# Weight conversion through PSUM, a third raw weight buffer, and a rearranged start in a fused attention and MoE kernel

## The chip, the cores and the metric

The kernel runs on one core of a Trainium2 chip. The time is the device time of one execution in microseconds. Three timed executions of the kernel before gave 914.54, 918.44 and 958.26 us; the median, 918.44 us, is the time before. The profile is of one further execution, which took 917.19 us.

## The reference

The kernel computes bucketed attention over 2 batches of 8 heads, 768 positions and 64 dimensions, and then two MoE-like layers with the same shapes, the second on the output of the first. Cut to what is computed:

```
q_bits = (q @ proj > 0); k_bits = (k @ proj > 0)            # 6 bits per position
mask   = bucket(q_bits) == bucket(k_bits)
scores = where(mask, q @ k.T / 8, -1e9)
attn   = exp(scores - max);  attn = attn / (sum(attn) + 1e-9)
x      = (attn @ v), heads side by side                      # 1536 x 512
h      = x @ w_in;  x = (s * relu(h)**2 + b) @ w_out         # w_in 512 x 2048
h      = x @ w2_in; out = (h * clip(h + 3, 0, 6) / 6) @ w2_out
```

q, k, v and proj come as float32. The four weight matrices come as float64 (8 bytes per element, 2 x 16 tiles of 128 x 512 for each layer), and the kernel itself turns them into float32.

## The kernel before, in words

**Precision.** Every operand of a matmul is split into a high part (a cast, on ACT) and a low part (a subtraction, on POOL or DVE), and three products are added. So each weight tile is cast (w_hi, L653, ACT), subtracted (w_lo, L659, POOL) and then used by twelve matmuls of 384 columns (mm, L681).

**Attention.** The work is cut into 4 units (batch, half of the queries) of 4 head pairs, 16 pairs g in all, and each pair into 6 slots. For a pair, k and q are loaded (load_k, load_q), cast (k_hi, q_hi, q_top) and split (k_lo, q_lo on POOL). The bucket bits of k and q are found by a small matmul (bits_mm, L381) and a comparison on DVE (bits, L390). The k bits are scaled by a large number on ACT (bits_big, L396), stored to DRAM (bits_out, L402), and fetched from there into rows 64 to 75 of the operand KA (bits_in, L413); the q bits go straight into QA in two small DMAs (L406). Rows 64 to 127 of QA and KA are first filled with 0 and 1 (ones_rows, L328 and L329, POOL). Score tiles S (qk, L460) are reduced to a row maximum by DVE (smax, L468). When a pair's twelve maxima are there, the transposed scores T are computed (st, L520), exponentiated and split (texp, t_hi on ACT, t_lo on POOL), multiplied with v (pv_mm, L549) and summed (den_mm, L560). The first unit's four pairs are loaded at the start of the program.

**The two layers.** There are 8 jobs of 32 weight tiles: both layers for each of the four units. In a job the first 16 tiles (the lower half) each make one block of the hidden layer: a PSUM bank is filled by 12 matmuls, then read by a chain of four steps that alternate between ACT and DVE (g_relu L692, g_prod L698, g_hi L705, g_lo L713 for the first layer; L700, L707, L716 stand in it for the second), and the bank is free when g_lo has ended. The last 16 tiles (the upper half) fill one bank per four tiles. Accumulators rotate over three banks: one of the ring mm, two of the ring mmx (function mring); the ring mm also holds the small matmuls' results of the first unit.

**The conversion.** In jobs 0 and 1 each weight tile is loaded raw (w_load, L613, 512 KB, two buffers wr), and made float32: ACT scales the upper words into a buffer wm (w_exp, L619) and writes the low half-words of the result wf (w_ends, L631), DVE writes the sign bits (w_ends, L633) and joins wm into wf (w_join, L638). wf is stored to DRAM (w_store, L644, 256 KB) and used; jobs 2 to 7 fetch it from there (L648). A raw buffer is free when L619, L631 and L633 have read it.

**What sets the order.** A planner in the program (class Plan) lists all steps with engine, expected duration, needs and buffer rings, and writes one fixed order for each engine's queue and for the DMA queue of SP (some DMAs go to ACT's queue). On the chip each engine works through its order and waits at the first step that isn't ready. A table of constants (P_BUFS ... AHEAD, WARM) and the durations in the add calls steer the planner.

**The warming block.** warm (L374) issues matmuls of 512 columns on a tile `idle` of zeros that nobody reads; WARM says how many.

Of the kernel before, what the change touches and what calls it, by code (L numbers as in the profile page):

```python
# [20 lines left out]
NB = 6  # L21
# [6 lines left out]
P_BUFS, PT_BUFS, WF_BUFS, WS_BUFS, WR_BUFS, WM_BUFS, AHEAD = 2, 3, 4, 3, 2, 1, 7  # L28
WARM = 8
# [196 lines left out]
def attn_moe_moe2(ctx, tc, qT, kT, vT, proj, cvec, eye, w1_in, w1_out, w2_in, w2_out, out):  # L226
# [21 lines left out]
    wm_p = ctx.enter_context(tc.tile_pool(name="wm", bufs=WM_BUFS))  # L248
# [18 lines left out]
    idle = const.tile([128, 512], F16, name="idle")  # L267
# [6 lines left out]
    eyes = const.tile([128, 390], F32, name="eyes")  # L274
    ident, own_slot = eyes[:, 0:128], eyes[96:96 + 2 * SPP, 384:390]
# [219 lines left out]
    def u_rows(g):  # L495
        fl = sm_p.tile([128, 128], F32, tag="fl", name="fl")
        nc.scalar.copy(fl[96:114], pd[g]["nr"][96:114, 0:128])
        pd[g]["fl"] = fl
# [118 lines left out]
    def w_exp(key):  # L617
        mt = wm_p.tile([128, 512], I32, tag="wm", name="wm")
# [111 lines left out]
    def o_store(j, d, key):  # L730
# [7 lines left out]
                 "vt": 4, "iv": 4, "pvs": 1, "U": 1, "ds": 1, "kH": 1, "qD": 1, "kHx": 1, "qDx": 1, "nx": 3, "nh": 2, "cols": 2, "fl": 3,  # L738
                 "o": 2, "r": 2, "wr": WR_BUFS, "wm": WM_BUFS, "wf": WF_BUFS, "wh": WS_BUFS, "wl": WS_BUFS})
# [35 lines left out]
    for g in range(NP):  # L775
# [15 lines left out]
        for nm in "kq":  # L791
            if nm == "q" or own:
# [7 lines left out]
                else:  # L800
                    add("ACT", t, 0.48, bits_big, (g,), needs=[("bits", g, nm)], gives=[("big", g)])
                    add("DMA", t, (0.45, 0.55), bits_out, (g, nm), needs=[("big", g)], gives=[("ks", g)], rel=[(o, (nm, g))])
# [175 lines left out]
```

## Time and profile before

| | |
|---|---|
| timed executions | 914.54, 918.44, 958.26 us |
| profiled execution | 917.19 us, its span 915.4 us |
| PE busy | 845.7 us, 92% of the span |
| ACT, POOL, DVE busy | 591.8, 593.5, 510.4 us |
| DMA | 136.71 MB, mean 149 GB/s |

The span is the stretch of the profiled execution from the first to the last instruction; the 1.8 us between it and the execution's time lie around it. Busy time of an engine is the sum of its instructions, and the rows of the section on the trace give it for stretches of the span. PE means the matmuls. The share of granted TensorE clock (PEclk) is 1.00 at full speed. The chain that ended last leads from the last instruction back to the first, at each step to what that step had waited for.

### The profile page before, as it was taken

How to read it: one execution, taken by the hardware profiler on the slowest of the kernel's cores; microseconds unless marked ns; L12 is line 12 of the kernel's file. 1: busy time of each engine (PE TensorE's matmuls, PEld its weight loads, DVE VectorE, ACT ScalarE, POOL GpSimd, SP SyncE). 2: the span in 40 equal slices, each digit the busy share in tenths (PEclk: the TensorE clock that was granted, in tenths of full speed). 3: DMA queues.
4: the chain of work that ended last, by engine and by line, in shares of the span. 5: the costliest groups of instructions: out<-in, count | busy, mean ns of one | idle time of the engine just before them, and what ended most of it. 6: DMA issues, size and time to landing. Idle time of an engine off the chain costs nothing.

```text
span 915.4 us, 15214 instructions
## 1 busy us (share of the span) xinstructions
PE 845.7 (92%) x5416; PEld 745.2 (81%) x5416; DVE 510.4 (56%) x845; ACT 591.8 (65%) x993; POOL 593.5 (65%) x396
## 2 busy tenths in 40 slices
PE   4998776997789989899999999999999999999998
PEld 1666456896778877899899887999988787999998
DVE  3688676889798878682554434540474532530520
ACT  5288757886898876475468575663777464753752
POOL 9387633587475777367757878566687665666664
PEclk9999899998898999899999999999999999999999
DMA  9634567778875575855533434344342222444342
GB/s 210 149 79 138 139 215 228 243 249 259 256 227 190 186 210 158 201 159 133 127 113 107 129 100 124 122 128 127 120 127 79 78 67 73 134 128 127 118 143 74
DMA packets 74843, 136.71 MB, mean 149 GB/s; under 512 B 20144, under 2 KB 30736, under 8 KB 74768
## 3 DMA queue, kind: packets, MB, share of 16 engines
q1 hardware_dynamic: 72834, 131.99, 49.1%
q10 hardware_dynamic: 1934, 3.76, 1.6%
q8 instruction: 42, 0.69, 0.3%
q14 instruction: 33, 0.27, 0.1%
HBM read 104.15 MB, written 21.54 MB: 137 GB/s over the span
## 4 chain that ended last, share of the span: by engine, by line
PE 72%; DMA 11%; DVE 9%; ACT 5%; issue 2%; SPq 1%; POOL 1%; ACTq 0%; DVEq 0%; POOLq 0%
PE mm L681 49%; PE S L460 7%; DMA wr<-w_in 6%; PE T L520 6%; PE pv L549 5%; DMA wr<-w_out 2%; DVE wf L638 1%; DVE nh L468 1%; PE S L560 1%; DVE wf L633 1%; ACT wf L631 1%; PE pv L581 1%; PE S L381 1%; DMA vP<-v_t 1%; ACT wm L619 1%
## 5 line engine op out<-in xcount | busy, mean ns | idle before, releaser
L659 POOL TENSOR_TENSOR wl<-wf,wh 128x512 fp32r<-128x512 f32 x256 | 339.9, 1330 | 223.8 <-ACT wh L653 182.1
L681 PE MATMUL mm<-X,wh 128*128 128x384 f32 x1024 | 271.6, 346 | 20.8 <-DVE G L713 13.0
L681 PE MATMUL mm<-G,wh 128*128 128x384 f32 x1024 | 269.5, 344 | 0.0
L653 ACT CAST wh<-wf 128x512 fp32r<-128x512 f32 x256 | 157.6, 617 | 93.0 <-PE mm L681 65.3
L539 POOL TENSOR_TENSOR pt<-P,pt 128x768 f16<-128x768 f32 x96 | 162.1, 1693 | 81.6 <-ACT pt L533 78.0
L681 PEld LDWEIGHTS mm<-X,wh 128*128 128x128 f32 x1024 | 189.1, 194 | 30.8 <-DVE G L713 17.1
L681 PEld LDWEIGHTS mm<-G,wh 128*128 128x128 f32 x1024 | 183.0, 188 | 13.9 <-issue 12.0
L681 PE MATMUL mm<-X,wl 128*128 128x384 f32 x512 | 175.1, 342 | 0.0
L681 PE MATMUL mm<-G,wl 128*128 128x384 f32 x512 | 173.1, 338 | 0.0
L468 DVE TENSOR_REDUCE nh<-S 128x1 f32<-128x384 f32 x192 | 103.9, 551 | 84.6 <-PE S L460 83.8
L526 ACT ACTIVATE P<-T 128x768 f32<-128x768 f32 x96 | 77.8, 810 | 40.5 <-PE T L520 36.3
L681 PEld LDWEIGHTS mm<-X,wl 128*128 128x128 f32 x512 | 99.1, 194 | 0.0
L681 PEld LDWEIGHTS mm<-G,wl 128*128 128x128 f32 x512 | 96.3, 188 | 0.4 <-POOL wl L659 0.4
L533 ACT CAST pt<-P 128x768 f16<-128x768 f32 x96 | 79.6, 831 | 7.6 <-PE pv L549 5.5
L460 PE MATMUL S<-KA,QA 76*128 76x384 f32 x192 | 75.5, 393 | 7.9 <-DVE nh L468 6.6
L638 DVE SCALAR_TENSOR_TENSOR wf<-wm,wf 128x512 int32<-128x512 int32 x64 | 66.2, 1034 | 14.9 <-ACT wm L619 12.9
L520 PE MATMUL T<-QA,KA 108*128 108x384 f32 x192 | 69.7, 363 | 3.9 <-ACT P L526 3.8
L631 ACT ACTIVATE wf<-wr 128x512 uint16<-128x512 uint16 x64 | 50.8, 794 | 31.2 <-issue 12.4
L460 PE MATMUL S<-KB,QB 128*128 128x384 f32 x192 | 69.3, 361 | 0.0
L549 PE MATMUL pv<-pt,vt 128*64 128x384 f16 x576 | 64.1, 345 | 4.6 <-DVE wf L638 4.5
L520 PE MATMUL T<-QB,KB 128*128 128x384 f32 x192 | 66.7, 348 | 0.0
L633 DVE TENSOR_SCALAR wf<-wr 128x512 uint16<-128x512 uint16 x64 | 57.8, 903 | 14.6 <-issue 5.9
(357 smaller groups left out, 975.4 us busy)
## 6 DMA issues: line engine op xcount, KB each, us to landing
wf<-w SPq DMA_DIRECT2D x188, 256.0 KB
wr<-w_in SPq DMA_DIRECT2D x32, 512.0 KB
wr<-w_out SPq DMA_DIRECT2D x32, 512.0 KB
w<-wf SPq DMA_DIRECT2D x63, 256.0 KB
KB<-KA SPq DMA_DIRECT2D x16, 384.0 KB
qD<-q_t SPq DMA_DIRECT2D x28, 192.0 KB
kH<-k_t SPq DMA_DIRECT2D x13, 384.0 KB
U<-ur SPq DMA_DIRECT2D x15, 192.0 KB
```

What stands on the lines that cost most here:

```text
L460: nc.tensor.matmul(out=sp[:, 0:NQ], lhsT=operand(g, Q)[0:n, h, 128 * t:128 * t + 128], rhs=operand(g, K)[0:n, h, NQ * j:NQ * j + NQ], star ...
L468: nc.vector.reduce_max(out=pd[g]["nh"][:, j, c:c + 1], in_=sd.pop((s, j))[:, 0:NQ], axis=AX.X, negate=True)
L520: nc.tensor.matmul(out=tp[:, j, 0:NQ], lhsT=operand(g, K)[0:n, h, c:c + 128], rhs=operand(g, Q)[0:n, h], start=(a == 0), stop=(a == 1))
L526: nc.scalar.activation(out=P, in_=td.pop((g, k))[:, :, 0:NQ], func=AF.Exp, scale=0.125)
L533: (nc.scalar.copy if THI(g) == "ACT" else nc.vector.tensor_copy)(pd[g][h][:, 0, 2 * i:2 * i + 2], pd[g]["P", k])
L539: e.tensor_tensor(out=pt[:, 1, 2 * i:2 * i + 2], in0=pd[g].pop(("P", k)), in1=pt[:, 0, 2 * i:2 * i + 2], op=ALU.subtract)
L549: nc.tensor.matmul(out=d["pv"][64 * h:64 * h + 64, 0:NQ], lhsT=vt[:, vc, 64 * h:64 * h + 64], rhs=d[h][:, a, c], start=(c == 0 and n == 0) ...
L633: nc.vector.tensor_scalar(out=f16[:, :, 1], in0=r16[:, :, 3], scalar1=0x8000, scalar2=None, op0=ALU.bitwise_and)
L638: nc.vector.scalar_tensor_tensor(out=wf, in0=wq[key]["mt"], scalar=3, in1=wf, op0=ALU.logical_shift_left, op1=ALU.bitwise_or)
L653: nc.scalar.copy(hi.rearrange("p a b -> p (a b)"), wq[key]["wf"])
L659: nc.gpsimd.tensor_tensor(out=lo.rearrange("p a b -> p (a b)"), in0=d["wf"], in1=d["hi"].rearrange("p a b -> p (a b)").bitcast(F32), op=AL ...
L681: nc.tensor.matmul(out=a, lhsT=w[:, k, :], rhs=src[k][:, xi, :], start=(k0 + k == 0 and p == 0), stop=(k0 + k == nk - 1 and p == 2))
```

## The change

Five things are changed.

- w_exp writes the scaled upper words into a PSUM bank of the ring mm in place of the SBUF buffer wm, which is gone. Accumulators of jobs 0 and 1 use the two banks of mmx alone; from job 2 on all three rotate as before.
- The raw weights have three buffers.
- For the first four pairs the k bits go from the tile `bits` straight into KA, in four DMAs of 12 x 384 words. They are still stored to DRAM, later, for the second unit with the same keys.
- The warming block comes in two parts, 16 matmuls after the first pair's bits and 6 after the second's, and works on the tile `eyes` in place of a tile of zeros.
- The constant rows of QA and KA are set by DVE in place of POOL.

The small buffer fl has one copy in another pool, the release of iv moves to a later step, and several durations that the planner assumes for DMAs and for w_join are changed, which reorders the program.

```diff
-P_BUFS, PT_BUFS, WF_BUFS, WS_BUFS, WR_BUFS, WM_BUFS, AHEAD = 2, 3, 4, 3, 2, 1, 7
-WARM = 8
+P_BUFS, PT_BUFS, WF_BUFS, WS_BUFS, WR_BUFS, AHEAD = 2, 3, 4, 3, 3, 7
+WARM = (16, 6)
...
-    idle = const.tile([128, 512], F16, name="idle")
+    idle = eyes.bitcast(F16)[:, 0:512]
...
     def ones_rows(e):
-        nc.gpsimd.memset(sets[e]["QA"][64:128].bitcast(F32), 0.0)
-        nc.gpsimd.memset(sets[e]["KA"][64:128].bitcast(F32), 1.0)
+        nc.vector.memset(sets[e]["QA"][64:128].bitcast(F32), 0.0)
+        nc.vector.memset(sets[e]["KA"][64:128].bitcast(F32), 1.0)
...
     def bits_in(g):
         u, hp = pairs[g]
+        if g < 4:
+            dst = operand(g, "KA").rearrange("p h n -> p (h n)").bitcast(F32)
+            for i in range(4):
+                queue[0].dma_start(out=dst[64:64 + 2 * NB, 384 * i:384 * i + 384], in_=pd[g]["kbt"][32 * i:32 * i + 2 * NB].bitcast(F32))
+            return
...
     def w_exp(key):
-        mt = wm_p.tile([128, 512], I32, tag="wm", name="wm")
+        mt = ps["mm"].tile([128, 512], F32, tag="mm", name="wm").bitcast(I32)
...
+    CONV = max(min(n for n, job in enumerate(jobs) if job[0] == m) for m in range(2))
+
     def mring(key):
         jn, i = key
         n = 20 * jn + (i if i < 16 else 12 + i // 4)
-        return "mm" if n % 3 == 2 else "mmx"
+        return "mm" if jn > CONV and n % 3 == 2 else "mmx"
...
-    add("PE", -80.0, 0.22 * WARM, warm, (WARM,), needs=[("qmm", 1), ("kmm", 1)], acq=[("pv", "w")], rel=[("pv", "w")], soon=-80.0)
+    for i, n in enumerate(WARM):
+        add("PE", -80.0, 0.22 * n, warm, (n,), needs=[("kmm", i), ("qmm", i)], acq=[("pv", ("w", i))], rel=[("pv", ("w", i))], soon=-80.0)
     for e in range(4):
-        add("POOL", e - 4.0, 1.4, ones_rows, (e,), gives=[("ones", e)])
+        add("DVE", 9.0 * e - 14.0, 2.0, ones_rows, (e,), gives=[("ones", e)])
...
-                add("DMA", tw - 4.0, (0.45, 1.46), w_load, (m, i, ck), needs=use, acq=[(wr, ck)], gives=[("wr",) + ck])
+                add("DMA", tw - 4.0, (0.6, 2.2), w_load, (m, i, ck), needs=use, acq=[(wr, ck)], gives=[("wr",) + ck])
...
-                add("DVE", tw, 1.09, w_join, (ck,), needs=[("we",) + ck, ("wd", 1) + ck], gives=[("wf",) + ck],
+                add("DVE", tw, 0.66, w_join, (ck,), needs=[("we",) + ck, ("wd", 1) + ck], gives=[("wf",) + ck],
```

**Order at the start, SP's queue.** Of before first (kb is the tile in DRAM that the k bits pass through, KB<-KA a copy within the operands, kH and kHx raw keys, qD and qDx raw queries, vP raw values):

```order
L355 DMA KB_153<-KA_151 64x1536
L355 DMA KB_157<-KA_155 64x1536
L402 DMA kb_121<-bits 128x384
L406 DMA QA_152<-bits 12x384 x2
L334 DMA kH<-k_t 64x1536
L342 DMA qD<-q_t 64x2x384 x2
L413 DMA KA_151<-kb_121 12x4x384
L402 DMA kb_122<-bits 128x384
```

And of the change:

```order
L354 DMA KB_149<-KA_147 64x1536
L413 DMA KA_147<-bits 12x384 x4
L405 DMA QA_148<-bits 12x384 x2
L333 DMA kH<-k_t 64x1536
L401 DMA kb_117<-bits 128x384
L354 DMA KB_153<-KA_151 64x1536
```

The fetch of the first pair's k bits stood behind a store and three loads; its four pieces now stand behind one copy, ahead of the q bits, and the store follows the next key load.

**Order at the start, DVE.** Of the change, where before only five small memsets stood ahead of the first bits (QA and KA are the operands of the first unit's pairs):

```order
L327 MEMSET QA_148 64x768
L328 MEMSET KA_147 64x1536
L327 MEMSET QA_152 64x768
L328 MEMSET KA_151 64x1536
L327 MEMSET QA_159 64x768
L328 MEMSET KA_158 64x1536
L389 TENSOR_SCALAR bits<-small,cv 128x384
L327 MEMSET QA_163 64x768
L328 MEMSET KA_162 64x1536
L389 TENSOR_SCALAR bits<-small,cv 64x384
L423 TENSOR_REDUCE am<-vP 128x1
```

Three pairs of memsets stand ahead of the first k bits and a fourth ahead of the first q bits.

**Order at the first raw loads, SP's queue.** Of before (ur and U are small tiles of the attention, w_0 the first converted tile in DRAM):

```order
L613 DMA wr<-w_in 128x1024 [waits DMAHW3_49]
L613 DMA wr<-w_in 128x1024 [waits DMAHW4_49]
L501 DMA ur_132<-fl 6x128 [waits DMAHW5_49,Activation_49]
L334 DMA kH<-k_t 64x1536 [waits DMAHW6_49,Pool_49]
L505 DMA U<-ur_131 128x1x384 [waits DMAHW7_49,DVE_49]
L613 DMA wr<-w_in 128x1024 [waits DMAHW0_49,DMAHW3_49,DVE_49,Activation_49]
```

And of the change:

```order
L617 DMA wr<-w_in 128x1024 [waits DMAHW1_49]
L617 DMA wr<-w_in 128x1024 [waits DMAHW2_49]
L617 DMA wr<-w_in 128x1024 [waits DMAHW3_49]
L509 DMA U<-ur_126 128x1x384 [waits DMAHW4_49,DVE_49]
```

Three raw loads now go out before one waits for DVE and ACT to have read a buffer; before there were two.

## Rows read from the trace of the kernel before

**Rows 1.** The page: PE's busy tenths in 40 slices; the chain by line.

```profile
PE   4998776997789989899999999999999999999998
PE mm L681 49%; PE S L460 7%; DMA wr<-w_in 6%; PE T L520 6%; PE pv L549 5%; DMA wr<-w_out 2%; DVE wf L638 1%; DVE nh L468 1%; PE S L560 1%; DVE wf L633 1%; ACT wf L631 1%; PE pv L581 1%; PE S L381 1%; DMA vP<-v_t 1%; ACT wm L619 1%
```

**Rows 2.** Busy time by stretch: PE, PEld, DVE, ACT, POOL, clock, DMA share, GB/s.

```profile
22.00:46.00 24.00, 23.83 (x72) 14.86 (x73) 16.27 (x36) 6.98 (x11) 9.86 (x5) 1.00 0.69 148
46.00:108.00 62.00, 56.67 (x450) 41.16 (x448) 49.15 (x92) 51.27 (x71) 48.92 (x28) 0.94 0.40 105
108.00:120.00 12.00, 6.54 (x89) 3.83 (x90) 6.42 (x10) 5.70 (x11) 6.04 (x4) 0.86 0.89 245
120.00:175.00 55.00, 41.75 (x211) 37.41 (x211) 41.26 (x72) 41.63 (x78) 20.18 (x14) 0.97 0.68 225
207.00:230.00 23.00, 17.95 (x144) 15.64 (x145) 21.14 (x24) 15.14 (x24) 17.77 (x10) 0.87 0.77 247
230.00:300.00 70.00, 58.52 (x338) 53.16 (x337) 58.77 (x94) 60.48 (x107) 39.58 (x25) 0.92 0.71 229
```

**Rows 3.** The same view of L631 alone (one per weight tile): ACT, clock, DMA.

```profile
120.00:175.00 55.00, 11.95 (x15) 0.97 0.68 225
230.00:300.00 70.00, 14.24 (x18) 0.92 0.71 229
```

**Rows 4.** The chain in order of time: start us, us, what.

```profile
11.02 0.52 ACT bits L396
...
16.61 4.93 DMA KA<-kb
...
21.78 1.62 PE S L460 x4
...
41.51 1.65 PE T L520 x4
...
44.44 2.41 PE T L520 x8
...
64.77 0.91 PE S L460 x4
...
191.53 2.12 PE mm L681 x12
```

**Rows 5.** The timeline at the start: start us, us, engine, line, what.

```profile
0.87 0.27 DVE L914 MEMSET idle<- 128x256 uint32 x1 [0.87 <-PEq L971]
6.89 0.62 DVE L390 TENSOR_SCALAR bits<-small,cv 128x384 fp32r<-128x384 f32 x1 [5.45 <-PE small L381]
8.88 3.44 POOL L358 TENSOR_TENSOR KB<-kH,KA 64x1536 fp32r<-64x1536 f32 x1
12.38 2.07 SPq L406 DMA_DIRECT2D QA<-bits  x2
17.52 3.60 PE L374 MATMUL pv<-idle 128*128 128x512 f16 x8
```

**Rows 6.** Waits of SP's DMA queue from 110 to 365: us, times, longest.

```profile
SPq L613 <- DVE wf L633: 62.3, 38, 5.8
```

**Rows 7.** Two DVE lines: ns (min/median/max), first and last start.

```profile
L713 DVE SCALAR_TENSOR_TENSOR G<-mm,cv,G x64: 596/617/620, 130.8 to 814.2; 128x384 fp32r<-128x384 f32 x64
...
L638 DVE SCALAR_TENSOR_TENSOR wf<-wm,wf x64: 673/692/3758, 94.2 to 357.5; 128x512 int32<-128x512 int32 x64
```

**Rows 8.** The timeline of three lower-half tiles of job 0, columns as above.

```profile
142.10 0.48 ACT L692 ACTIVATE r__1690<-mm 128x384 f32<-128x384 f32 x1
...
142.98 0.51 ACT L692 ACTIVATE r__1704<-mm 128x384 f32<-128x384 f32 x1
...
145.19 0.62 DVE L713 SCALAR_TENSOR_TENSOR G<-mm,cv,G 128x384 fp32r<-128x384 f32 x1 [0.34 <-ACT G L705]
...
145.86 0.61 PE L681 MATMUL mm<-X,wh 128*128 128x384 f32 x2 [1.13 <-DVE G L713]
...
149.78 0.60 DVE L713 SCALAR_TENSOR_TENSOR G<-mm,cv,G 128x384 fp32r<-128x384 f32 x1
```

More of the change, by code (lines that the diff above doesn't have):

```diff
@@ L495, in u_rows @@
     def u_rows(g):
-        fl = sm_p.tile([128, 128], F32, tag="fl", name="fl")
+        fl = raw_p.tile([128, 128], F32, tag="fl", name="fl")
         nc.scalar.copy(fl[96:114], pd[g]["nr"][96:114, 0:128])
@@ L801, in attn_moe_moe2 @@
                     add("ACT", t, 0.48, bits_big, (g,), needs=[("bits", g, nm)], gives=[("big", g)])
-                    add("DMA", t, (0.45, 0.55), bits_out, (g, nm), needs=[("big", g)], gives=[("ks", g)], rel=[(o, (nm, g))])
+                    add("DMA", t + (6.0 if g < 4 else 0.0), (0.45, 0.55), bits_out, (g, nm), needs=[("big", g)], gives=[("ks", g)], rel=[(o, (nm, g), 2 if g < 4 else 1)])
             if nm == "k":
-                add("DMA", t, (0.45, 0.2), bits_in, (g,), needs=[("ks", g if own else g - 4)] + free + [("ones", at(g))], gives=[("km", g)])
+                add("DMA", t, (2.2, 0.2) if g < 4 else (0.45, 0.2), bits_in, (g,), needs=[("big", g) if g < 4 else ("ks", g if own else g - 4)] + free + [("ones", at(g))], gives=[("km", g)],
+                    rel=[("r", ("k", g), 2)] if g < 4 else [])
         ops = [("km", g), ("qm", g), ("kd", g, 0), ("kd", g, 1), ("qd", g, 0), ("qd", g, 1), ("qh", g), ("kh", g)]
@@ L808, in attn_moe_moe2 @@
             tv = t + VLEAD
-            add("DMA", tv, (0.45, 1.1), load_v, (g,), needs=[("pv", g - 4)] if u else [], acq=[("vP", g)], gives=[("v", g)])
+            add("DMA", tv, (0.6, 1.7), load_v, (g,), needs=[("pv", g - 4)] if u else [], acq=[("vP", g)], gives=[("v", g)])
             add("DVE", tv, 2.6, v_scale, (g,), needs=[("v", g)], acq=[("iv", g)], gives=[("vs", g)])
@@ L812, in attn_moe_moe2 @@
             add("DVE", tv, 1.2, v_lo, (g,), needs=[("vh", g)], gives=[("vl", g)], rel=[("vP", g)])
-            add("TR", tv, (0.62, 1.34), v_tr, (g,), needs=[("vl", g)], acq=[("vt", g)], gives=[("vt", g)], rel=[("vhl", g)])
+            add("TR", tv, (0.62, 2.0), v_tr, (g,), needs=[("vl", g)], acq=[("vt", g)], gives=[("vt", g)], rel=[("vhl", g)])
         for i in range(SPP):
@@ L846, in attn_moe_moe2 @@
             rel=[("pt", (g, 0), 2), ("pt", (g, 1), 2)])
-        add("ACT", b + 5.6, 0.48, pv_cp, (g,), needs=[("pv", g)], acq=[("pvs", g)], gives=[("pc", g)], rel=[("iv", g - 4)] if u % 2 else [])
+        add("ACT", b + 5.6, 0.48, pv_cp, (g,), needs=[("pv", g)], acq=[("pvs", g)], gives=[("pc", g)])
         add("ACT", b + 6.2, 0.33, den_cp, (g,), needs=[("dn", g)], acq=[("ds", g)], gives=[("ds", g)], rel=[(br, ("d", g))])
@@ L875, in attn_moe_moe2 @@
                         acq=[] if h else [("wf", ck)], gives=[("wd", h) + ck] + ([] if h else [("wi",) + ck]), rel=[(wr, ck, 3)])
-                add("DVE", tw, 1.09, w_join, (ck,), needs=[("we",) + ck, ("wd", 1) + ck], gives=[("wf",) + ck],
+                add("DVE", tw, 0.66, w_join, (ck,), needs=[("we",) + ck, ("wd", 1) + ck], gives=[("wf",) + ck],
                     rel=[(wm, ck)])
                 last = [("wf", ck, 2)]
-                add("DMA", tw, (0.45, 0.73), w_store, (m, i, ck), needs=[("wf",) + ck], gives=[("ws", m, i)], rel=last)
+                add("DMA", tw, (0.55, 1.1), w_store, (m, i, ck), needs=[("wf",) + ck], gives=[("ws", m, i)], rel=last)
             else:
-                add("DMA", t - 4.0, (0.45, 0.73), w_fetch, (m, i, key), needs=[("ws", m, i)] + past(jn, i, AHEAD) + before("wi", jn, i), acq=[("wf", key)],
+                add("DMA", t - 4.0, (0.55, 1.1), w_fetch, (m, i, key), needs=[("ws", m, i)] + past(jn, i, AHEAD) + before("wi", jn, i), acq=[("wf", key)],
                     gives=[("wf",) + key, ("wi",) + key])
@@ L913, in attn_moe_moe2 @@
     with tc.manual_schedule():
-        nc.vector.memset(idle, 0.0)
         nc.vector.memset(three, 3.0)
```

15 lines of the change are left out of this document (7 added, 8 removed).

## The prediction, made before the changed kernel ran

> **What bounds it now.** I read the page first, then busy time by stretch, then the chain, and last the waits of the stretches where PE is not full. In the slices PE stands at 9 nearly throughout the second half, and below it in the first slice and in many of slices 4 to 17 [rows 1]. So the last 500 us are PE's own work, which the change leaves as it is, and there is nothing to win there. The chain by line says what the first half waits for: behind PE's lines stand the landings of raw weights, 6% and 2%, some 73 us of 915 [rows 1].
>
> By stretch, PE is idle 5.5 us in 108 to 120, 13.2 in 120 to 175, 5.1 in 207 to 230 and 11.5 in 230 to 300, 35 us together; the mean clock there (0.86, 0.97, 0.87, 0.92) gives away another 1.7 + 1.7 + 3.0 + 5.6 = 12 us [rows 2]. These **47 us** are all that a better conversion could return. No engine is full in 120 to 175: PE, ACT and DVE all stand near 41.6 of 55 us [rows 2]. They wait in turn for one cycle. SP's queue held raw loads back 62.3 us, in 38 waits, for DVE's reading of a raw buffer [rows 6]: with two buffers a load can't start until the tile two before it is read.
>
> The start is a separate matter. The first S matmul begins at 21.78, right after the k bits' way through DRAM (issued at 16.61, 4.93 us to land) [rows 4]. Then four S matmuls take 1.62 us, four T matmuls at 41.51 take 1.65 and eight T at 44.44 2.41 us; at 64.77 four S take 0.91 [rows 4]. PE is thus on the lower of its two levels, 1.2 GHz, until about 46, though the granted clock of 22 to 46 reads 1.00 [rows 2]; the level shows in the pace alone. The eight warming matmuls, 3.60 us from 17.52 [rows 5], did not raise it. What did was the T and S row that ran without a gap from 41.51 on.
>
> **The change, part by part.** The sum is made against the profiled execution, 917.2 us, 0.1% under the median of the timed runs, 918.4.
>
> *Constants on DVE.* POOL's first subtraction starts at 8.88, behind eight memsets [rows 5]; these go, and POOL has the first pair's rows ready earlier than anybody wants them. DVE's 256-word memset takes 0.27 us [rows 5]; by length 768 and 1536 words are 0.8 and 1.6 us. Three pairs ahead of the first k bits are 7.3 us from about 1.2, so these come at 8.5 and not at 6.89 [rows 5]: **1.6 us later**. The first q bits wait for the fourth pair, until about 11.5.
>
> *k bits straight in.* ACT scales the bits in 0.52 us [rows 4], so the first of the four pieces is issued near 9.7. Two q-bit DMAs took 2.07 us to issue [rows 5], so a piece costs about 1 us of SP, the four 4 us, and the q bits go out at 13 to 15. They then are last. The first S needs the first q piece, issued by 14. Its landing lies between nothing and the 4.93 us of the DRAM fetch on the same loaded queues [rows 4]; I take 3.5, nearer to the row, since the same loads are in flight. First S: about 17.5, so **4.3 us earlier** (bounds: 14 to 20, 2 to 7.8 us earlier).
>
> *Warming.* 16 matmuls at the pace of the old block, 0.45 us, are 7.2 us; they follow the q bits' matmul, which waits for the k bits to free its bank at 9.1 and is taken as four S matmuls, 1.6 us [rows 4]; so they start near 10.7 and end near 17.9, when the first S is about ready: no cost (at most 0.4 us). The block is longer than the gapless row that began at 41.51 and had raised the clock by about 46, so I expect 2.4 GHz at the first S. Then two S tiles cost DVE's two reductions, not 1.62 us on PE. Most of the 19.7 us from the first S to the first T is S at that pace [rows 4]. Reductions and other DVE work fill 16.27 of 24 us there [rows 2], so no more than 7.7 us can be had; half of that I leave to the loads of the later pairs, which the change doesn't quicken (DMA share 0.69 there [rows 2]). I take **3 us** (0 to 7.7). After it POOL, ACT and DVE carry the unit, 49 to 51 of 62 us [rows 2]; they start earlier and end earlier. Start: 4.3 + 3 = **7 us**.
>
> *Third raw buffer.* In 120 to 175 a tile takes 55 / 15 = 3.67 us, in 230 to 300 70 / 18 = 3.89 us [rows 3]. The same buffer cycle (two tiles, 7.3 us) over three buffers would be 2.45 us, so the load stops being the limit. What is next: DMA at 0.68 x 3.67 = 2.5 us per tile, ACT and PE 41.7 / 15 = 2.8 [rows 2, 3], and the accumulators.
>
> *Upper words in PSUM.* L638 takes 0.69 us as a median but up to 3.76, while L713, which reads one operand from PSUM, never leaves 596 to 620 ns [rows 7]. A joined tile of 512 columns with one PSUM operand is 617 x 512 / 384 = 0.82 us at most. The median gains nothing; the long ones, which stand between a raw load and its use, go. On ACT the same number of words are written. I count nothing for it alone: it removes jitter from the cycle that the third buffer already frees.
>
> *Two accumulator banks.* This is the price. A lower-half bank is held 2.12 us by PE [rows 4] and then by the chain: of the tile relu'd at 142.10, until 145.81, 3.7 us [rows 8]. With two banks a tile takes (2.12 + 3.7) / 2 = **2.9 us**. PE waited for that chain with three banks too (1.13 us at 145.86 [rows 8]).
>
> So the lower half of job 0 goes from 3.67 to about 3.1 us per tile (the 2.9 with some slack): 15 x 0.57 = 9 us. In 207 to 230, half of the 8 us of idle and clock: 4 us. In 230 to 300 ACT needs 60.48 / 18 = 3.36 us per tile [rows 2, 3], so at best 3.6: 18 x 0.29 = 5 us. Together **18 us**. The small edits (fl, iv) are hidden: fl's one copy is used once per pair, of which the first unit has four in 62 us.
>
> Sum: 917.2 - 7 - 18 = **892 us**.
>
> **Weighed against a rule.** The four pieces and two q-bit DMAs were priced above by their issue. The Trainium skill, SBUF — State Buffer, section "The DMA setup-cost knee", says every transfer pays a roughly fixed 2 us however small, and its rules for kernel authors ask for one DMA instead of several. No row here times such a piece alone. If the fixed parts added up, four pieces would cost 8 us, an estimate from that page, and the start would win nothing: the sum would be 899 by the page and 892 by the rows. The same outcome, as a mechanism of this kernel, is the third rival.
>
> **The rivals.**
>
> *Banks take the load's place (22%).* If ACT and DVE, still in a fixed order, hold the chain near 5.2 us, a lower-half tile takes (2.12 + 5.2) / 2 = 3.67, as now. For it: in the same stretch the tile relu'd at 142.98 kept its bank until 150.38, 7.4 us [rows 8]. Against: part of that was ACT and DVE waiting for raw weights. Then 7 us of the start and perhaps 3 of the upper half remain: 907.
>
> *More comes back (12%).* If ACT and DVE never stall on raw weights, the chain shortens too, PE closes up and keeps its clock: two thirds of the 47 us, 31, and 7: 879. Against it: ACT is at 60.48 of 70 us [rows 2].
>
> *The start gains nothing (8%).* The small DMAs queue behind the loads (as KA<-kb did for 4.93 us), or PE falls back to 1.2 GHz before the S tiles run densely. Then 917 - 18 = 899. For it: the clock column drops where PE had idled, 0.86 in 108 to 120 [rows 2].
>
> *Slower by the banks (8%).* If the chain were as long as the worst one throughout, (2.12 + 7.4) / 2 = 4.76 us per lower-half tile, 32 tiles of jobs 0 and 1 would lose 1.1 us each, 35 us, against 7 won: 945. It decides the sign of the whole from a chain of about 5.7 us on ((2.12 + 5.7) / 2 is 0.24 more than now, 8 us in 32 tiles); over 2% slower needs 6.8 us.
>
> **How the numbers follow.** My forecast, 892, has the remaining 50%; its own range is 882 to 903 (start 2 to 14 us, conversion 12 to 21). The range takes in most of the 907 and the 879: 876 to 910, leaving out the slow case, the far side of the 907 and of the 879, about 2 in 10. A change below 2% (18 us, about what a measurement of this kernel can tell) means 900 to 937. Faster by more: four fifths of the forecast (0.40), the 879 (0.12) and half of the 899 (0.04): 0.56. Slower by more: 0.08. The rest, 0.36, lies within.
>
> **What would show it.** The first S near 17.5 with four S matmuls in about 1.1 us; the first T near 34; raw loads at about 3 us per tile in job 0's lower half; no long joins; PE's waits there mostly for G of the second tile before. Wrong would be: S still near 1.6 us per four, a first S after 20, or lower-half tiles at 3.7 us and more with PE waiting for G, which is the bank rival.

## The result, and the profile after

The changed kernel takes **927.75 us** (median; 922.16 to 928.6), the kernel before 916.62 beside it: a ratio of 1.0114, with 1.0066 to 1.0163 as its 95% interval. The forecast was 892, its range 876 to 910. The change makes the kernel slower, by some 11 us, 1.1%. All ratios below are to the kernel before on the same chip (its median there was 916.13 to 919.48 us), with such an interval in brackets; times in us come from different chips, so compare the ratios. Ratios use the fast executions alone, and the one of 958.26 us is not among them.

The page of the changed kernel, as in [rows 1] (span 920.4 us, profiled execution 922.16). That execution is the fastest of the kernel's five and only 5 us slower than the profiled one of before, so the trace shows about half of the 11 us:

```profile
PE   6697797999888899999998899999999899999998
...
PE mm L687 51%; PE T L524 7%; PE S L464 6%; PE pv L553 6%; DVE nx L476 2%; DMA KB<-KA 1%; DVE nh L472 1%; PE S L564 1%; DVE wf L637 1%; DVE mk L482 1%; DMA wr<-w_out 1%; PE pv L585 1%; PE S L380 1%; DVE cols L484 1%; ACT wf L635 1%
```

The landings of raw weights have shrunk from 6% and 2% to about 1%, as forecast. New in the chain are nx, mk and cols: DVE operations on six values per row. In the second half of the slices, where before had 9 throughout, there are now some of 8. Busy time by stretch, as in [rows 2], and two stretches far behind the conversion:

```profile
22.00:46.00 24.00, 15.63 (x62) 10.59 (x61) 12.69 (x29) 9.76 (x13) 11.63 (x5) 0.64 0.87 152
46.00:108.00 62.00, 52.18 (x429) 39.49 (x428) 50.25 (x87) 47.60 (x70) 45.23 (x27) 0.92 0.60 151
108.00:120.00 12.00, 9.28 (x50) 5.79 (x49) 9.31 (x14) 8.39 (x14) 7.70 (x5) 0.72 0.42 124
120.00:175.00 55.00, 46.38 (x285) 41.20 (x284) 41.40 (x75) 42.19 (x81) 21.87 (x17) 0.97 0.66 217
207.00:230.00 23.00, 20.86 (x155) 18.62 (x156) 18.03 (x27) 17.14 (x28) 13.25 (x10) 0.93 0.66 197
230.00:300.00 70.00, 59.55 (x357) 51.99 (x356) 58.56 (x95) 57.85 (x101) 43.04 (x28) 0.90 0.76 235
...
500.00:510.00 10.00, 5.11 (x26) 4.79 (x25) 8.30 (x8) 4.99 (x7) 9.63 (x6) 0.78 0.49 136
540.00:550.00 10.00, 7.86 (x38) 7.39 (x39) 5.82 (x10) 3.43 (x6) 6.08 (x5) 0.83 0.47 112
```

PE is fuller by 4.6 us in 120 to 175, by 2.9 in 207 to 230 and by 1.0 in 230 to 300. But busy time alone hides work that was put off. So I counted, in each trace, the S, T, pv, den and mm matmuls begun by a given time, and weighed each with its pace at the full clock (S, T and mm 0.177 us, pv 0.092, den 0.023). The difference to the kernel before is the **lead** in us of PE's work. Every trace here has all 5,184 of these matmuls, and at the end the lead equals the difference of the spans within 0.4 us; but each line is one execution, and executions of one kernel differ by 5 us and more.

| at us | 46 | 108 | 175 | 230 | 300 | 360 | 410 | 500 | 584 | 780 |
|---|---|---|---|---|---|---|---|---|---|---|
| the change | 0.0 | -2.5 | +2.5 | +3.0 | +0.8 | +3.0 | +9.7 | +5.8 | **-6.4** | -4.6 |
| change, small tiles in PSUM | 0.0 | -2.5 | +1.8 | +4.6 | +5.4 | +6.8 | +14.0 | +12.7 | +12.7 | +20.2 |
| the same, late transposing | +2.7 | -0.4 | +9.7 | +12.0 | +10.6 | +11.2 | +20.0 | +17.6 | +18.8 | +26.4 |
| before, new DMA costs | +1.8 | -4.1 | -1.1 | -2.5 | -2.5 | -5.9 | -6.9 | -8.3 | -10.1 | -7.3 |
| before, new DMA costs, small tiles in PSUM | +0.7 | -0.5 | +8.0 | +9.9 | +2.9 | +0.8 | +7.1 | +7.4 | +7.8 | +14.3 |
| before, small tiles in PSUM | -0.4 | -0.4 | -1.9 | +2.5 | +0.4 | +0.7 | -4.2 | -3.0 | -5.7 | +0.7 |

The first line tells the result: nothing from the start, 3.0 us by 360, when the last weight tile has been joined (357.5), 6.7 more by 410, and 16.1 us lost between 410 and 584, where the forecast saw only PE's own work. Of the last 84 us of that stretch PE is idle 8.1 us, at a mean clock of 0.94; in the kernel before it was busy for all 84, at 1.00. What PE waits for there is in the next two views. First the timeline of DVE and POOL at 500 us (start, duration, engine, line, operation):

```profile
501.73 3.48 POOL L357 TENSOR_TENSOR KB<-kH,KA 64x1536 fp32r<-64x1536 f32 x1 [0.21 <-ACT KA L351]
501.76 3.47 DVE L476 TENSOR_TENSOR nx<-nh 128x6 f32<-128x6 f32 x1
505.26 0.17 DVE L482 SCALAR_TENSOR_TENSOR mk<-nx 128x6 f32<-128x6 f32 x1
505.28 1.82 POOL L367 TENSOR_TENSOR QB<-qD,QB 64x768 fp32r<-64x768 f32 x1
505.46 1.66 DVE L483 TENSOR_SCALAR cols<-mk 128x6 fp32r<-128x6 f32 x1
...
507.24 1.24 DVE L485 TENSOR_SCALAR cols<-nx 128x6 fp32r<-128x6 f32 x1
508.41 1.65 POOL L543 TENSOR_TENSOR pt<-P,pt 128x768 f16<-128x768 f32 x1
508.53 0.77 PE L490 MATMUL S<-eyes,cols 128*114 128x128 f32 x2 [4.89 <-DVE cols L485]
```

An operation of 0.17 us takes 3.47: it begins 0.03 us behind POOL's subtraction (k_lo of a later pair) and ends with it. mk, in the gap between two of POOL's instructions, takes its 0.17 us; cols (L483) is caught behind q_lo in the same way, and cols (L485) behind a weight tile's subtraction. PE stands 4.89 us. At 571 us mk takes 4.63 us, through two of POOL's instructions. In the whole trace 30 of the 80 operations of the chain take more than 0.3 us, and each of the 30 ends within 0.03 us of the end of an instruction of POOL; in the kernel before it is 29 of 80. The Trainium skill, SBUF — State Buffer, section "Who interferes with whom", has the rule: a DVE instruction with two SBUF inputs and a GpSimd instruction that reads SBUF exclude each other, as do a DVE instruction in a two-port mode and a GpSimd instruction, and the second blocks for the whole of the first. The trace agrees to 0.03 us. The same section lets a DVE instruction with at most one SBUF input, in no such mode, run freely beside GpSimd; experiment 1 rests on that.

Second, the waits of PE (us, times, longest), and the length of the chain's operations and of the joins (ns min/median/max). The first wait in the kernel before, and then three of the change:

```profile
PE S L486 <- DVE cols L481: 12.8, 6, 4.9
```

```profile
PE S L490 <- DVE cols L485: 19.4, 9, 4.9
PE mm L687 <- DVE G L722: 8.8, 6, 2.9
...
PE mm L687 <- DVE G L719: 7.5, 7, 3.6
```

```profile
L476 DVE TENSOR_TENSOR nx<-nh x16: 142/631/3472, 30.3 to 744.3; 128x6 f32<-128x6 f32 x16
...
L482 DVE SCALAR_TENSOR_TENSOR mk<-nx x16: 166/167/4628, 30.5 to 746.0; 128x6 f32<-128x6 f32 x16
...
L642 DVE SCALAR_TENSOR_TENSOR wf<-wm,wf x64: 628/691/694, 84.3 to 357.5; 128x512 int32<-128x512 int32 x64
```

The 80 operations on six values take DVE 52 us together, 38 in the kernel before. The joins, with one input now in PSUM, never leave 628 to 694 ns (up to 3,758 before [rows 7]): the edit cured there what it left in the chain of the maxima.

The start, from the timeline and from the chain (start, us, what):

```profile
8.55 0.62 DVE L389 TENSOR_SCALAR bits<-small,cv 128x384 fp32r<-128x384 f32 x1
...
9.75 3.25 SPq L413 DMA_DIRECT2D KA<-bits  x4
...
10.64 5.32 PE L373 MATMUL pv<-eyes 128*128 128x512 f16 x16
15.61 0.54 PE L464 MATMUL S<-KA,QA 76*128 76x384 f32 x1
15.99 0.34 PE L464 MATMUL S<-KB,QB 128*128 128x384 f32 x1
16.17 0.34 PE L464 MATMUL S<-KA,QA 76*128 76x384 f32 x1
...
20.00 1.66 SPq L450 DMA_TRANSPOSE vt<-vhl  x1
...
24.65 9.33 ACTq L413 DMA_DIRECT2D KA<-bits  x4
...
26.28 8.12 SPq L341 DMA_DIRECT2D qDx<-q_t  x2
...
34.02 1.47 ACT L351 CAST KA<-kHx 64x1536 fp32r<-64x1536 f32 x1 [8.68 <-DMA KB<-KA]
...
34.60 0.66 PE L464 MATMUL S<-KA,QA 76*128 76x384 f32 x1 [4.94 <-DMA KA<-bits]
```

```profile
20.70 12.53 DMA KB<-KA
...
40.51 1.28 PE T L524 x4
```

The first S comes at 15.61 instead of 21.78, and the first four take 1.07 us instead of 1.62. Then the second pair's S stands until 34.60 (33.11 before), the granted clock of 28 to 44 is 0.50, and the first T is only 1.0 us earlier. Behind the transposing transfer of 20.00 what was issued next on both queues lands, or is accepted, at 33 to 35.

### The profile page after: what moved, and what is told of

Same layout as the page of the kernel before. It is cut to its first block, busy times and chain, and to the rows that moved or that the text cites. A ratio compares the mean times of both kernels' runs of the same rounds, so it can differ in the third digit from the quotient of the medians.

```text
span 920.4 us, 15259 instructions
## 1 busy us (share of the span) xinstructions
PE 845.2 (92%) x5430; PEld 747.9 (81%) x5430; DVE 514.0 (56%) x852; ACT 589.7 (64%) x993; POOL 576.6 (63%) x388
## 4 chain that ended last, share of the span: by engine, by line
PE 74%; DVE 12%; DMA 6%; ACT 5%; issue 2%; POOL 0%; SPq 0%; ACTq 0%; DVEq 0%; POOLq 0%
PE mm L687 51%; PE T L524 7%; PE S L464 6%; PE pv L553 6%; DVE nx L476 2%; DMA KB<-KA 1%; DVE nh L472 1%; PE S L564 1%; DVE wf L637 1%; DVE mk L482 1%; DMA wr<-w_out 1%; PE pv L585 1%; PE S L380 1%; DVE cols L484 1%; ACT wf L635 1%
## 5 line engine op out<-in xcount | busy, mean ns | idle before, releaser
L663 POOL TENSOR_TENSOR wl<-wf,wh 128x512 fp32r<-128x512 f32 x256 | 332.6, 1302 | 235.1 <-ACT wh L657 205.5
L687 PE MATMUL mm<-G,wh 128*128 128x384 f32 x1024 | 272.4, 347 | 1.7 <-DVE G L722 1.7
L657 ACT CAST wh<-wf 128x512 fp32r<-128x512 f32 x256 | 157.8, 618 | 99.7 <-PE mm L687 67.5
L543 POOL TENSOR_TENSOR pt<-P,pt 128x768 f16<-128x768 f32 x96 | 161.2, 1683 | 66.9 <-ACT pt L537 62.3
L687 PEld LDWEIGHTS mm<-G,wh 128*128 128x128 f32 x1024 | 185.2, 190 | 15.4 <-issue 12.9
L464 PEld LDWEIGHTS S<-KA,QA 76*128 76x128 f32 x192 | 38.0, 198 | 31.8 <-DVE nh L472 15.8
L357 POOL TENSOR_TENSOR KB<-kH,KA 64x1536 fp32r<-64x1536 f32 x14 | 48.8, 3483 | 19.8 <-ACT KA L351 19.7
```

Source lines behind the costliest of these rows:

```text
L357: nc.gpsimd.tensor_tensor(out=operand(g, "KB")[0:64], in0=pd[g]["k"], in1=operand(g, "KA")[0:64].bitcast(F32), op=ALU.subtract)
L464: nc.tensor.matmul(out=sp[:, 0:NQ], lhsT=operand(g, Q)[0:n, h, 128 * t:128 * t + 128], rhs=operand(g, K)[0:n, h, NQ * j:NQ * j + NQ], star ...
L543: e.tensor_tensor(out=pt[:, 1, 2 * i:2 * i + 2], in0=pd[g].pop(("P", k)), in1=pt[:, 0, 2 * i:2 * i + 2], op=ALU.subtract)
L657: nc.scalar.copy(hi.rearrange("p a b -> p (a b)"), wq[key]["wf"])
L663: nc.gpsimd.tensor_tensor(out=lo.rearrange("p a b -> p (a b)"), in0=d["wf"], in1=d["hi"].rearrange("p a b -> p (a b)").bitcast(F32), op=AL ...
L687: nc.tensor.matmul(out=a, lhsT=w[:, k, :], rhs=src[k][:, xi, :], start=(k0 + k == 0 and p == 0), stop=(k0 + k == nk - 1 and p == 2))
```

## Experiments

**1. The small tiles out of SBUF.** In the change and in the kernel before, each in its own order, one half of nh, nx and mk go into the unused columns of the pv bank, so that no operation of the chain reads two SBUF tiles. Every engine works through the same order as without the edit, apart from the second minimum added for each pair. The warming block writes 384 columns in place of 512; in the change, the lead up to 108 us is the same with either.

```diff
+    pvb = ps_v.tile([128, 512], F32, name="pvb")
-            pd[g]["nh"] = sm_p.tile([128, 2, SPP], F32, tag="nh", name="nh")
+            pd[g]["nh"] = [pvb[:, 400 + 6 * (g % 2):406 + 6 * (g % 2)], sm_p.tile([128, SPP], F32, tag="nh", name="nh")]
...
+        pd[g]["nx"] = pvb[:, 416:422]
+        pd[g]["ny"] = sm_p.tile([128, SPP], F32, tag="nx", name="ny")
+        for nx in (pd[g]["nx"], pd[g]["ny"]):
+            nc.vector.tensor_tensor(out=nx, in0=pd[g]["nh"][0], in1=pd[g]["nh"][1], op=ALU.min)
...
+        mk = pvb[:, 432:438]
```

Expected of the change with it: 

> The changed kernel in its own order, with the small tiles of the maxima (one half of nh, nx, mk: 6 values per row) in the free quarter of the pv bank of PSUM, so that no tiny operation reads two tiles of SBUF; one operation more for each pair, and the warm-up writes 384 instead of 512 columns. Theory A: DVE's tiny operations are held up by POOL's use of SBUF (up to 4.6 us instead of 0.17); now all take under 0.3 us, the waits of PE for cols (19.4 us before the nx products) shrink below 10, and the time falls by 8 to 12 us to 916 to 920. Rival B: the chain is late because the maxima themselves come late in this order: the operations get short but the time falls by 3 us at most, 925 or more.

Expected of the kernel before with it: 

> The same small tiles in PSUM, in the kernel before with its own order. Theory A (POOL holds DVE up there too, but less of it is bare: PE waits 12.8 us for cols): 3 to 6 us faster, 911 to 914. Rival B: within 2 us of 917.

Measured: the change **899.24 us, 0.9813 [0.9748, 0.9879]**; the kernel before 914.7, 0.9967 [0.9930, 1.0003]. The 96 operations (one more per pair) take 15.9 us in the change, none over 0.17, though 81 of them lie wholly within an instruction of POOL. Change with small tiles in PSUM, timeline and PE's wait:

```profile
494.63 3.54 POOL L358 TENSOR_TENSOR KB<-kH,KA 64x1536 fp32r<-64x1536 f32 x1
...
494.72 0.17 DVE L479 TENSOR_TENSOR pvb<-pvb,nh 128x6 f32<-128x6 f32 x1
494.93 0.17 DVE L479 TENSOR_TENSOR ny<-pvb,nh 128x6 f32<-128x6 f32 x1
495.13 0.17 DVE L485 SCALAR_TENSOR_TENSOR pvb<-pvb,ny 128x6 f32<-128x6 f32 x1
```

```profile
PE S L493 <- DVE cols L488: 1.1, 1, 1.1
```

POOL's blocking is shown, and it is worth more than theory A said: 28 us of the change, 19 of them in the lead by 584 us and 6 between 584 and 780, where the last pairs have such chains too. PE's waits for cols account for 19 of the 28 (20.4 to 1.1 us, with those of the ring `small`). For the kernel before the gain is 3 us, the low end of theory A, and the interval takes in rival B too: PE's waits for cols go there as well (13.2 to 1.4 us), but in its order little comes of it, and waits for G, the products' chain, grow from 19.3 to 23.4 us. The larger of these:

```profile
PE mm L684 <- DVE G L716: 17.5, 8, 6.4
```

(13.0 before, on L713.)

**2. The parts, each planned anew, in both places of the small tiles.** The start part alone in the kernel before; everything but the start part; and only the numbers that the planner assumes for DMA issue and transfer (one of them below), with the later release of iv, which move instructions and change none. Then the same with the small tiles in PSUM, and the change without its conversion.

```diff
-                add("DMA", tw - 4.0, (0.45, 1.46), w_load, (m, i, ck), needs=use, acq=[(wr, ck)], gives=[("wr",) + ck])
+                add("DMA", tw - 4.0, (0.6, 2.2), w_load, (m, i, ck), needs=use, acq=[(wr, ck)], gives=[("wr",) + ck])
...
```

Expected, start alone: 

> The kernel before with the start part of the change alone (warming block, first key bits straight into the operand, constants set by DVE); conversion, third buffer and DMA costs stay as before. Theory A (from the two traces): the first pair gains some 6 us but the second pair loses them again behind ACT's queue, and by 108 us the array has done 6 us less work than before: 916.6 + 6 = 922 us, with first S near 16 us and first T of the second pair late. Rival B (the step on record): the start gains 7 us and what comes later keeps it: 909 us. Either can be moved by up to 5 us where the new order falls otherwise in the later jobs.

All but the start: 

> The change without its start part: conversion through PSUM, third buffer, two banks and the new DMA costs, but the warm-up of 8 products, key bits through DRAM and constants by POOL as before. Theory A: without the start's loss of 6 us the gain of the conversion (12 us) and the loss in the third unit's attention at 500 to 584 us (14 us) are left: 927.8 - 6 = 922 us, first S near 22 us. Rival B: the start was a gain of 7 us, so without it 934 us. Rival C: the loss at 500 to 584 us hangs on the order that the planner happened to find for the whole change and goes with any new order: 927.8 - 6 - 14 = 908 us.

Only the DMA costs: 

> The kernel before, with the planner's assumed costs for DMA issue and transfer set to those of the change (and the release of one small tile counted later); every operation and buffer is as before, only the order of the instructions can move. Theory A (an order that leaves the chain of the maxima bare costs time by itself): several us either way, 916.6 + 5 to 916.6 + 14 if these numbers make the order that loses at 500 to 584 us. Rival B (the order after the conversion does not matter, PE is full there): 916.6 within 2 us.

Only the DMA costs, small tiles in PSUM: 

> The kernel before with the planner's DMA costs of the change, a new order and nothing else, which ran 9 us longer than before (926), now with the small tiles in PSUM. Theory A (a new order costs because it leaves the chain of the maxima bare where POOL holds DVE): the loss goes, 907 to 915 us. Rival B (the new order loses by other things, as the places of the transfers): 920 to 926.

All but the start, small tiles in PSUM: 

> The changed kernel with the small tiles in PSUM but without the start part (8 warming products, key bits through DRAM, constants by POOL), planned anew. Theory A (orders cost little once POOL cannot hold up the chain of the maxima, and the start part gains what shows at 46 us at most): 899 + 0 to 5 us, 899 to 904. Rival B (the start part loses some 6 us, as the trace of the change showed at 80 us): 892 to 895. Rival C (the order alone still moves it): over 908.

All but the conversion, small tiles in PSUM: 

> The changed kernel with the small tiles in PSUM but with the conversion of the kernel before (wm in SBUF, two raw buffers, banks for the products of the first two jobs in threes as before), planned anew. Theory A (with the chain of the maxima out of the way the conversion bounds 120 to 300 us, and the change's conversion is worth what the step on record said or somewhat less): 899 + 10 to 18 us, 909 to 917, with PE's waits for G near 23 us as against 14.6. Rival B (the conversion part is worth little, the maxima were all): 897 to 903.

| ratio to before | small tiles in SBUF | in PSUM |
|---|---|---|
| kernel before, its order | 1 | 0.9967 [0.9930, 1.0003] |
| only DMA costs (new order) | 1.0101 [1.0019, 1.0184] | **0.9803 [0.9753, 0.9853]** |
| DMA costs and conversion | 1.0143 [1.0060, 1.0227] | 0.9845 [0.9789, 0.9900] |
| DMA costs and start | | 0.9876 [0.9819, 0.9933] |
| the whole change | 1.0114 [1.0066, 1.0163] | 0.9813 [0.9748, 0.9879] |
| start, old DMA costs | 1.0073 [1.0034, 1.0112] | |

Read across, the two kernels of a row have the same order on every engine, and each of three new orders loses 1.0 to 1.4% with the small tiles in SBUF and wins 1.6 to 2.0% with them in PSUM: 3% each time, against 0.3% in the old order. So a new order, by the planner's numbers alone, costs as much as the whole change does (925.96 us, theory A in size), and that loss goes with POOL's hold on the chain: 902.46 us, more than theory A gave it.

It is not the same loss at the same place, though. With the DMA costs alone the lead is down to -10.4 at 371 us, and between 410 and 584 it falls by 3.2 us, against 16.1 in the change. That the chain of the maxima, held by POOL, costs the change its time is shown by experiment 1; that the DMA costs, and not the other edits, made the change's own order bare there is not shown.

Read down, the operations of the start and of the conversion together are worth 0.1% in either column, over the new order alone. The single steps in PSUM lie between -0.6% and +0.7%, each with its own new order and with overlapping intervals, so what each part is worth by itself stays open within some 6 us. Without its start the change, tiles in PSUM, took 903.13 us, as theory A had it; without its conversion 905.21, between the theories; the whole takes 899.24.

In SBUF, two expectations failed. The start alone (926.01, 1.0073) is slower, as theory A said, but not by its mechanism: at 108 us the lead is +0.4, not -6. All but the start (930.66) was to take 922; it is near rival B's 934, which held the start for a gain, though another order explains it as well.

**3. Operations changed, order kept.** The order of the kernel before, written down and replayed: once with the operations of the start part, once with a third raw buffer. And the change with two raw buffers (small tiles in PSUM, planned anew).

```diff
-        for fn, a, on in plan.order():
+        for x in ORDER.split(","):
+            o = ranked[abs(int(x)) - 1]
...
-P_BUFS, PT_BUFS, WF_BUFS, WS_BUFS, WR_BUFS, WM_BUFS, AHEAD = 2, 3, 4, 3, 2, 1, 7
+P_BUFS, PT_BUFS, WF_BUFS, WS_BUFS, WR_BUFS, WM_BUFS, AHEAD = 2, 3, 4, 3, 3, 1, 7
```

Expected, start: 

> The kernel before with the start part of the change (blocks of 16 and 6 warming products, first key bits straight into the operand, constants set by DVE), and every instruction in the order of the kernel before, on every engine and queue (only the two warming blocks stand behind the query bits of the first and of the second pair). Theory A (new orders cost, not the operations): what the start wins stays, 2 to 5 us: 912 to 915 us, and the later jobs look as before. Rival B (the operations of the start themselves lose it: four small transfers for each pair, DVE's constants): at 108 us no more products are done than before, 917 to 922 us.

Third buffer: 

> The kernel before with a third raw weight buffer alone, every instruction in the order of the kernel before (the place comes from the constant tile as warm-up operand and from the u rows, as in the change). Theory A (the step on record: SP waits 62.3 us for a free raw buffer, and the cycle of load and conversion sets the pace of 207 to 300 us): the waits of SP fall below 30 us and the time falls by 4 to 9 us to 908 to 913. Rival B (the queue's order and the other operations set the pace): SP waits elsewhere, under 2 us gained, 915 to 919.

Two buffers in the change: 

> The changed kernel with the small tiles in PSUM and two raw weight buffers instead of three, planned anew; the rest of the conversion as in the change. Without the whole conversion part it took 905, with it 899. Theory A (the third buffer is the larger part of what the conversion gives): 903 to 908. Rival B (the two banks and the upper words in PSUM are): 897 to 901.

Measured: start 1.0014 [0.9965, 1.0064]; third buffer 0.9967 [0.9931, 1.0002]; two buffers in the change 904.02 us, 0.9841 [0.9777, 0.9905]. The start's operations neither win nor lose in the old order: rival B, with a lead of 1.1 us at 108. The third buffer alone is worth 3 us (none to 6 by the interval), between the theories. With two buffers the change came out within theory A's times, but by the ratio it can't be told from three (0.9813). Kernel before with the third buffer, SP's waits in 110 to 365 (62.3 us in [rows 6]) and the chain of 142 to 176 us by line:

```profile
SPq L646 <- DVE wf L640: 125.9, 51, 5.9
...
SPq L615 <- DVE wf L635: 0.8, 1, 0.8
```

```profile
by line: PE mm L683 25.1%; DMA wr<-w_in 13.7%; issue 11.7%; DMA wr<-w_out 11.5%; DVE wf L640 10.8%; ACT wm L621 6.1%; DVE G L715 5.3%; POOL wl L661 5.2%; ACT wf L633 4.9%; DVE mm L700 3.9%; DVE QA L494 2.8%; ACT wh L655 2.4%; DVE wf L635 1.
```

The queue's wait has moved, as rival B said, from the raw buffer to the store of a joined tile (52.0 us before). In the kernel before, raw landings were 30.0% and 24.5% of that chain. Products, joins (both inputs in SBUF) and ACT have stepped in. The pace of job 0's lower half, from the first relu to the sixteenth, goes from 3.40 to 3.34 us per tile only; in the change it is 3.15. With the DMA costs alone, two buffers and the old conversion, it is 2.94. Its conversion counts, as in [rows 3]:

```profile
120.00:175.00 55.00, 12.26 (x16) 0.97 0.78 236
230.00:300.00 70.00, 12.72 (x16) 0.90 0.76 237
```

In that kernel SP waits longer than ever for the raw buffer (108.2 us in all, 67.5 before), and yet the lower half of job 0 is faster; 230 to 300 has two conversions less than before. So the length of that wait does not tell the pace. In the change itself, with its three buffers, the wait has not gone either; SP's wait there in 110 to 365:

```profile
SPq L617 <- DVE wf L637: 59.2, 33, 5.4
```

**4. The planner told the truth.** Tiles left in SBUF; the two steps of the maxima entered with times as they occur, in the change and in the kernel before.

```diff
-        add("DVE", A[SPP * g + SPP - 1] + 1.9, 0.12, both, (g,), needs=allmx, acq=[("nx", g)], gives=[("mx", g)], rel=[("nh", g)])
+        add("DVE", A[SPP * g + SPP - 1] + 1.9, 0.7, both, (g,), needs=allmx, acq=[("nx", g)], gives=[("mx", g)], rel=[("nh", g)])
...
-        add("DVE", a + 2.0, 0.7, nx_split, (g,), needs=[("mx", g)], acq=[("cols", g)], gives=[("nc", g)], rel=[("nx", g)])
+        add("DVE", a + 2.0, 2.4, nx_split, (g,), needs=[("mx", g)], acq=[("cols", g)], gives=[("nc", g)], rel=[("nx", g)])
```

Expected, change: 

> The changed kernel with its tiles as they are (small tiles in SBUF), but the planner is told that the two steps of the maxima take 0.7 and 2.4 us instead of 0.12 and 0.7, and makes its order with that. Theory A (the loss is an order that leaves no work of PE between the last maximum and its product, for lack of the true time): PE's waits for cols fall from 19.4 us below 10, and the time to 908 to 917. Rival B (no order covers it, or a new order loses elsewhere): 922 to 932.

Kernel before: 

> The kernel before, its order made with 0.7 and 2.4 us for the two steps of the maxima instead of 0.12 and 0.7; nothing else. Theory A (the missing time is a fault of the planner that lies in the kernel before too, and its order was one of the better ones by luck): 903 to 913 us. Rival B (its order covers the chain already, a new one gains nothing without the change's other parts): 914 to 922.

Measured: the change 902.68 us, 0.9851 [0.9783, 0.9918]; the kernel before 918.12, 0.9998 [0.9957, 1.0038], rival B. Two numbers win back most of what the PSUM tiles do. But PE's waits for cols are still 11.8 us, against the "below 10" expected, and the chain's operations take 65 us: its lead at 371 is 8.8 us, that of the change 3.0. The time, 902.68, is below what theory A gave. So part of the gain is another order altogether, and theory A is only half confirmed.

**5. The transposing transfer at the start.** The change with small tiles in PSUM and its order replayed, the first transposing put behind the loads of the first four pairs (what waits for its buffer, such as v_hi of the second pair and the second transposing, moves back with it); in a second kernel also the second pair's v_scale put later.

```diff
 load_k(3) on SP
-v_tr(0) on SP
 k_shift(2) on ACT
...
 load_k(4) on SP
 bits_in(2) on SP
+v_tr(0) on SP
```

Expected: 

> The changed kernel with the small tiles in PSUM, and its first transposing transfer (vt<-vhl, issued at 20 us) put behind the loads, shifts and bits of the first four pairs on SP's queue; what waits for its buffer (v_hi, v_lo of the second pair, the next load of v, its scaling and transposing) moves back with it, all else keeps its order. Theory T: from 20 to 34 us that transfer holds what both queues issued behind it (KB<-KA lands after 12.5 us, KA<-bits and qDx after 8 to 9 us), so the second pair's S starts at 34.6 to 35.5 us; without it S goes on near 29 us and the time falls by 4 to 6 us from 899 to 893 to 895. Rival Q: those transfers are slow by themselves (four small ones for each pair, or ACT's queue), S still starts after 33 us and less than 2 us is gained, 897 to 901.

With v_scale later: 

> The changed kernel with the small tiles in PSUM and the late transposing transfer (891 us), and the seven operations of v's scaling for the second pair (25 to 27.4 us on DVE, ahead of two maxima on which S waits 3.9 us) put behind the first pair's maxima. Theory A: S of the second pair goes on up to 3 us earlier and the time falls by 1 to 3 us to 888 to 890. Rival B: the second pair's S waits for KA<-bits at the same place, no change, 891.

Measured: **891.17 us, 0.9737 [0.9676, 0.9798]**; with v_scale later 896.35, 0.9735 [0.9687, 0.9784], the same. With the late transposing, timeline and chain, and last the transposing transfer in the chain of the kernel without this edit:

```profile
24.71 3.67 ACTq L416 DMA_DIRECT2D KA<-bits  x4
...
26.51 3.07 SPq L344 DMA_DIRECT2D qDx<-q_t  x2
...
35.81 1.56 SPq L453 DMA_TRANSPOSE vt<-vhl  x1
...
39.61 0.94 ACT L441 ACTIVATE vhl<-vP,sc 128x768 f16<-128x768 f32 x1 [4.79 <-DMA vt<-vhl]
```

```profile
36.71 1.28 PE T L529 x4
```

```profile
19.98 14.52 DMA vt<-vhl
```

Without this edit the k bits' pieces also take 3.67 us to issue (9.33 in the change), but qDx goes out at 34.11 only, when the transposing transfer has nearly landed, and S of the second pair at 35.55; now they do at 26.51 and 29.93, and the first T comes 3.8 us earlier than in the change. Theory T holds. The lead grows by 7.9 us until 175, above the 4 to 6 expected; the ratios, 0.9813 and 0.9737, say 7 us, with overlapping intervals. v_scale was not what held the rest (rival B). This kernel beats both: 2.6% below the kernel before.

## Why the prediction was wrong, point by point

- **"The last 500 us are PE's own work, which the change leaves as it is"** failed, and it is the step that cost the sign: a lead of 9.7 us at 410 becomes one of -6.4 at 584. The diff changes the planner's numbers, so every job gets another order. In the old one little hung on the chains of the maxima (3 us, experiment 1); in the new one PE stands bare before them while POOL holds DVE: 12.2 us between 500 and 584, 28 us in all (experiment 1). A page in which PE reads 9 says that the order covers the waits, not that there are none.
- **What the change removes, adds and moves** was costed for operations only. The planner's DMA costs, ten lines of the diff with the release of iv, were priced at nothing, not even by their bounds. Alone they cost as much as the whole change, though largely at other places, and with the chain out of POOL's reach they win as much (experiment 2).
- **The gains were mis-sized too.** By 300 us, where the forecast has its whole 25 us in, the lead is 0.8. So without the loss behind 410 the profiled execution would still have stood at about 907, its lead of 9.7 us at 410 and no more.
- **Third raw buffer, 2.45 us per tile instead of the 7.3 us cycle**: in the kernel before with a third buffer the waits of SP went and the pace stayed, 3.34 us per tile for 3.40; in the change they stayed, 59.2 us (experiment 3). The step took the longest wait of a queue for the limit. In the kernel with only the DMA costs that wait is longer and the tile of job 0's lower half shorter.
- **Conversion, 18 us**: from 108 us to the last join the lead grows by 5.5 us; with the start it is worth 0.1% over its order. By stretch: 207 to 230 has 2.9 us more of PE and a better clock, about the 4 forecast, but the lead from 175 to 230 grows by 0.5 only; 230 to 300 has nothing of the 5. Job 0's lower half came to 3.15 us per tile by its relus, as forecast (3.1), but it had stood at 3.40 and not at the 3.67 counted in 120 to 175: 0.25 us gained, not 0.57. What holds 230 to 300 stays open: no run changed ACT's or DVE's load there.
- **Two banks**: PE did wait for the chain behind a bank (up to 3.6 us, for G of L719), yet for G in all it waits 16.3 us against 19.3 before. Neither bank rival decided.
- **Upper words in PSUM**, counted at nothing: right in mechanism, no long joins. The same reading was not carried to the one other chain with the same trouble, whose operations stood in the trace of before with medians of 0.16 to 0.40 us and up to 1.78.
- **Start, 7 us**: the first S (17.5 forecast, 15.61) was better and its pace right (four in 1.07 us, 1.1 forecast), the DVE delay of 1.6 us exact. The first T (34 forecast, 40.51) was wrong: the 3 us were given to S running faster, and the loads behind the second pair were not followed through the new queue order, where the transposing transfer had moved ahead of them (20.00 instead of 24.71). By the lead the start won nothing (0.0 at 46). If the fixed part that the Trainium skill, SBUF — State Buffer, section "The DMA setup-cost knee", gives to a transfer had added up to 8 us over four pieces, an estimate from that page, the first S would have been late; the rows do not show that: from the first piece's issue at 9.75 to S is 5.9 us, q bits included.
- **The rivals** all moved inside the same terms. The third had the start right in part, for the second pair: its small transfers wait behind others (9.33 us), and PE falls back to the lower level, 0.50 from 28 to 44 us, though behind the first pair's S and not before it. The one on the slow side needed banks; none had the order itself as its mechanism.

## What to carry to other kernels

Where a planner writes the order, an edit of its costs is an edit of the whole program: price it by the waits that the present order covers, and look at stretches far from the edit. Before such a change, search the trace for operations whose maximum is many times their median; they are the places where a new order can fall through. Here putting one input where POOL cannot block it was worth 3% in each of three new orders and 0.3% in the old one. And a queue that waits is not a limit until the pace behind it moves.

## What the runs showed of the hardware

- A DVE operation on 128x6 with two SBUF inputs that POOL holds up ends within 0.03 us of the end of POOL's instruction (3.47 us behind one of 3.48, and 4.63 through two). With one input in PSUM and one in SBUF it keeps 0.17 us through a 3.54 us subtraction.
- The one-input operations cols of L483 and L485, from SBUF to SBUF, are caught too (1.66 and 1.24 us); from PSUM they are not.
- A transposing transfer issued behind the loads landed about 3.8 us behind its issue (35.81 to 39.61). Issued among the loads it took 14.52 us (19.98 to 34.50), and plain transfers issued after it on both queues came little or no earlier (KB<-KA of 20.70 in the change after 12.53 us, at 33.2).
- The granted clock reads 1.00 for 22 to 46 us in the kernel before, where four S matmuls take 1.62 us, and 0.64 in the change, where the first four take 1.07: at the start the pace of the rows tells the level, the column does not.
